# Three queues for the last stores of a decode block: block 0 through GpSimd, block 1 as two 16-row stores

## The chip, the cores and the metric

The kernel runs on one core of a Trainium2 chip. The metric is the device time of one execution in microseconds. Before the change the median of 3 runs is 263.7 us (263.6 to 263.76).

## The reference

One decode step for 8 sequences: a layer norm, attention of 32 query heads over 4 KV heads and the last 1024 cached positions, an output projection with a residual, then a second layer norm and a gated feed-forward part with its own residual. All numbers are float32.

```
W = min(4096, max(256, Sk // 4))                       # 1024
q = layernorm(x) @ wq                                  # 8 x 4096: 32 heads of 128
p = softmax(q . k[last W] * Dh**-0.5)                  # 8 query heads share one KV head
h = x + (p . v[last W]) @ wo                           # 8 x 1024
n = layernorm(h)
h2 = h + (gelu(n @ w_gate) * (n @ w_up)) @ w_down      # 8 x 1024, the output
```

## The kernel before

Every weight and cache entry is read once, 111 MB in all, in a packed order: twelve units of 8 MB go in turn into two halves of SBUF (`wbuf`), then the rest of the down projection in pieces that shrink towards the end. TensorE multiplies each chunk by a few stationary columns. Four groups of 32 PSUM partitions hold four quarters of the 1024 output columns, so the result stands as 128 partitions x 256 columns (`o_fin`): partition group j has columns 256j to 256j + 255. Of each group of 32 partitions 8 carry the eight sequences that are wanted; the host picks them out after the launch.

The end of the program matters here. The last row block of `w_down` comes in two column blocks, of 160 and 96 columns per group (`ENDS`, L32). For each, four matmuls (L472) and one VectorE add (L475) give the block's part of `o_fin`. `done[i]` is the semaphore value that says block i's add is over. `move` (L95) issues one DMA from a named engine's queue with a semaphore that counts to 16 when the data is written. The list `sent` (L486) stores the two blocks: block 0 from SyncE, block 1 from ScalarE. `EDGES` (L34) says which partitions are stored: 24 to 104, that is 80 rows, in which the wanted rows are the first 16 and the last 16.

After its store ScalarE counts up `issued` (L493). SyncE waits for that (L494), clears the semaphores of the whole program in two range clears (L498), and then waits for each store's semaphore and sets it back (L500). SyncE's last wait ends the program. An engine's queue is in order: what stands behind a waiting instruction waits as well. GpSimd's last instruction is a copy at L429 (`singles`), 12 us before the end.

Of the kernel before, what the change touches and what calls it, by code (L numbers as in the profile page):

```python
# [2 lines left out]
F32 = mybir.dt.float32  # L3
# [5 lines left out]
B = 8  # L9
D = 1024  # L10
# [6 lines left out]
QW = D // NQ  # L17
# [13 lines left out]
ENDPARTS = (2, 1)  # L31
ENDS = (160, 96)  # L32
AHEAD = 3
EDGES = ((24, 104),)  # L34
PAD = 128


# [8 lines left out]
class Flow:  # L46
# [48 lines left out]
    def move(self, name, out, src, *waits, engine="sync", sem=None):  # L95
        s = self.sem(name) if sem is None else sem
        self.start(engine, lambda e: e.dma_start(out, src), waits).then_inc(s, 16)  # L97
        return s, 16


def decode_block(nc, x, units, dn, tails, ends, outs):

    fl = Flow(nc)
    run, move = fl.run, fl.move
# [3 lines left out]
    def sb(name, *shape):  # L108
        return nc.alloc_sbuf_tensor(name, list(shape), F32).ap()
# [37 lines left out]
    def half_b(k, h=1):  # L147
        return at_mark["b", k, h]
# [5 lines left out]
    for u in range(UNITS):  # L154
        k, i = divmod(u, 2)
# [7 lines left out]
    for i, (n, sem) in enumerate(zip(PARTS, (go[0], *go_later[1:]))):  # L163
        c0 = (q0 - EARLY) * D
# [4 lines left out]
    c0 = 0  # L169
    for i, n in enumerate(ENDPARTS):  # L170
        here = move(f"we{i}", wbuf[1][:, c0:c0 + n * D], tails[i], half_b(nb - 1))
# [6 lines left out]
    blocks = []  # L178
    a = 0
    for i, (n, src) in enumerate(zip(ENDS, ends)):  # L180
        t = wbuf[1][:, c0:c0 + NQ * n]
# [8 lines left out]
        out=ident, in_=ident, compare_op=ALU.not_equal, fill=1.0, base=0,  # L190
# [14 lines left out]
    for i, g in enumerate(go_later):  # L205
        run("gpsimd", lambda e: e.memset(note[:, i:i + 1], 0.0), gives=(g, GATE[i] * (passes - 1)))

    own = sb("own", P, HB)
    own_ok = run("vector", lambda e: e.tensor_reduce(
        out=own, in_=ident.rearrange("p (a b h) -> p b a h", b=HB, h=REP), axis=AX.XY,  # L210
# [88 lines left out]
    for hf in range(2):  # L299
        done = (half_a, half_b)[hf]  # L300
# [26 lines left out]
    for hf in range(2):  # L327
        done = (half_a, half_b)[hf]
# [3 lines left out]
            out=nmax, in_=sums[hf], axis=AX.X, op=ALU.max, negate=True), done(1))  # L332
# [12 lines left out]
    for hf in range(2):  # L345
        done = (half_a, half_b)[hf]
        o_sb = sb(f"o{hf}", P, DH)
        tok = None
        for h in range(2):
            o3 = sums[hf][:, h * N:(h + 1) * N].rearrange("p (b d) -> p b d", b=HB)  # L350
            for b in range(HB):
                end = h == 1 and b == HB - 1
                out = source[:, hf * DH:(hf + 1) * DH] if end else o_sb
# [39 lines left out]
    for k, n in enumerate(SETS):  # L393
# [16 lines left out]
        t = turned[:, 0:N].rearrange("p (i m) -> p i m", m=P)  # L410
# [24 lines left out]
    for ch in range(2):  # L435
        p0 = 32 * (2 + ch)
# [31 lines left out]
    o_fin = sb("o_fin", P, QW)  # L468
    done = []
# [10 lines left out]
    with nc.body("never", valid_engines=both):  # L480
# [3 lines left out]
    nc.switch_bb("through")  # L484

    sent = [  # L486
        move(f"out{i}_{k}", outs[i][k], o_fin[p0:p1, c0:c0 + n], done[i], engine=("sync", "scalar")[i])
        for i, (c0, n, t, here) in enumerate(blocks) for k, (p0, p1) in enumerate(EDGES)
    ]


    issued = fl.sem("issued")
    nc.scalar.sem_inc(issued, 1)  # L493
    nc.sync.wait_ge(issued, 1)  # L494
    late = [s.num for s, val in sent]
    for group in ([s.num for s in fl.sems if s.num < min(late)], [issued.num]):
        assert group == list(range(group[0], group[0] + len(group)))
        nc.sync.sem_clear(range(group[0], group[-1] + 1))  # L498
    for s, val in sent:
        nc.sync.wait_ge(s, val).then_inc(s, -val)  # L500


# [86 lines left out]
```

## Time and profile before

| | us |
|---|---|
| median of 3 runs | 263.7 |
| the profiled execution | 263.75 |
| its span, first to last instruction | 262.3 |
| TensorE busy | 142.3 (54%) |
| VectorE busy | 43.8 (17%) |
| ScalarE busy | 13.5 (5%) |
| GpSimd busy | 8.6 (3%) |
| mean DMA rate | 424 GB/s |

The span is the time between the first and the last instruction of the profile; the profiled execution's own time is 1.45 us more. Over most of the span the DMA engines are busy with weights, and the compute engines follow them. A store's row in the profile shows only its issue. Its data moves later, on the DMA engines, and its semaphore counts later still; "to landing" is the time from the issue's start to that count.

### The profile page before, as it was taken

To read this page: it belongs to the slowest core of one execution; us is meant where nothing else is said; L and a number is where in the kernel's file an instruction comes from. 1 tells how busy PE (TensorE), PEld (TensorE's weight loads), DVE (VectorE), ACT (ScalarE), POOL (GpSimd) and SP (SyncE) were. 2 spreads that over 40 slices of the span, in tenths; PEclk is the share of its full clock that TensorE was granted. 3 is DMA by queue.
4 is the path that set the end of the run, shared out by engine and by line. 5 is a ranking of instruction groups with operands and counts; after the bars stand their busy time and mean duration, and the time that the engine had idled before them with its cause. 6 is when DMAs were issued, how large, how long until landed. Compare 5 with 4: busy or idle time off the path is not lost. (4 is left out here: it accounts for less than half of the span.)

```text
span 262.3 us, 2264 instructions
## 1 busy us (share of the span) xinstructions
PE 142.3 (54%) x972; PEld 45.6 (17%) x972; DVE 43.8 (17%) x115; ACT 13.5 (5%) x19; POOL 8.6 (3%) x20
## 2 busy tenths in 40 slices
PE   0025705926806937607918408827609709309996
PEld 0021201211202322102202102122103202002332
DVE  0340200240110140400410100254100300100342
ACT  1000000000030010000000200000300000200000
POOL 6000100100000000100100000000000000000000
PEclk9999975985965965975986966965957956956999
DMA  8997997999799799979979998997999899799895
GB/s 320 485 460 340 480 480 320 480 480 460 340 480 480 320 480 480 460 340 480 480 320 480 480 450 350 480 480 320 480 480 450 350 480 480 320 440 480 375 422 215
DMA packets 2800, 111.27 MB, mean 424 GB/s; under 512 B 408, under 2 KB 616, under 8 KB 880
## 3 DMA queue, kind: packets, MB, share of 16 engines
q1 hardware_dynamic: 2688, 111.20, 98.4%
q10 hardware_dynamic: 112, 0.06, 0.1%
HBM read 111.18 MB, written 0.08 MB: 424 GB/s over the span
## 5 line engine op out<-in xcount | busy, mean ns | idle before, releaser
L232 PE MATMUL sum<-w,still 128*32 128x512 f32 x832 | 116.6, 723 | 95.9 <-PEq L219 95.9
L232 PEld LDWEIGHTS sum<-w,still 128*32 128x32 f32 x832 | 32.5, 130 | 176.4 <-issue 176.3
L250 PE MATMUL turned<-ident,source 128*128 128x128 f32 x64 | 11.1, 330 | 20.8 <-PEq L219 20.8
L250 PEld LDWEIGHTS turned<-ident,source 128*128 128x128 f32 x64 | 8.8, 169 | 26.1 <-issue 26.1
L245 PE MATMUL turned<-y_sb,add 128*32 128x512 f32 x24 | 11.3, 592 | 0.9 <-PEq L219 0.9
L331 DVE TENSOR_REDUCE nmax<-sum 128x1 f32<-128x1024 f32 x2 | 2.4, 1224 | 28.4 <-PE sum L232 28.4
L406 DVE TENSOR_TENSOR up<-up,sum 128x512 f32<-128x512 f32 (+1 forms) x2 | 1.4, 685 | 34.1 <-PE sum L232 34.1
L302 DVE TENSOR_SCALAR q<-sum 128x512 f32<-128x512 f32 x2 | 1.4, 692 | 25.5 <-PE sum L232 25.5
L287 DVE COPY still<-turned 128x1024 f32<-128x1024 f32 x4 | 4.7, 1220 | 4.3 <-PE turned L250 4.3
L396 DVE TENSOR_TENSOR gate<-gate,sum 128x512 f32<-128x512 f32 (+1 forms) x2 | 1.4, 686 | 23.6 <-PE sum L232 23.6
L358 DVE SCALAR_TENSOR_TENSOR o<-sum,share,o 128x128 f32<-128x128 f32 x12 | 4.2, 351 | 4.2 <-PE sum L232 3.8
L355 DVE TENSOR_SCALAR o<-sum,share 128x128 f32<-128x128 f32 x2 | 0.7, 351 | 23.9 <-PE sum L232 23.9
L362 POOL MEMSET still<- 128x1024 f32 x2 | 1.9, 951 | 76.0 <-PE sum L232 76.0
L333 ACT ACT_TABLE_LOAD x1 | 1.3, 1283 | 60.4 <-DVE nmax L331 60.4
L245 PEld LDWEIGHTS turned<-y_sb,add 128*32 128x32 f32 x24 | 2.6, 110 | 8.7 <-issue 8.7
L307 POOL MEMSET still<- 128x1024 f32 x2 | 1.9, 956 | 45.7 <-PE sum L232 45.7
L375 DVE TENSOR_TENSOR y_sb<-y_sb,sum 128x512 f32<-128x512 f32 x1 | 0.7, 687 | 15.8 <-PE sum L232 15.8
L373 ACT COPY y_sb<-sum 128x512 f32<-128x512 f32 x1 | 0.6, 586 | 50.7 <-PE sum L232 50.7
L333 ACT ACTIVATE source<-sum,nmax 128x1024 f32<-128x1024 f32 x2 | 2.2, 1113 | 17.1 <-PE turned L250 17.1
L374 DVE TENSOR_TENSOR y_sb<-y_sb,sum 128x512 f32<-128x512 f32 x1 | 0.7, 687 | 14.3 <-PE sum L232 14.3
L318 DVE COPY still<-turned 128x16 f32<-128x16 f32 x32 | 2.7, 165 | 2.1 <-PE turned L250 2.1
L429 POOL COPY singles<-at 128x128 f32<-128x128 f32 x1 | 0.7, 664 | 71.4 <-DVE at L411 71.4
(66 smaller groups left out, 44.7 us busy)
## 6 DMA issues: line engine op xcount, KB each, us to landing
w<-dn SPq DMA_DIRECT2D x1, 6144.0 KB, 24.5
w<-dn SPq DMA_DIRECT2D x1, 2048.0 KB, 29.1
w<-tails SPq DMA_DIRECT2D x1, 1024.0 KB, 12.0
w<-tails SPq DMA_DIRECT2D x1, 512.0 KB, 12.9
w<-ends SPq DMA_DIRECT2D x1, 320.0 KB, 13.3
w<-units SPq DMA_DIRECT2D x12, 29.3
w<-ends SPq DMA_DIRECT2D x1, 192.0 KB, 13.3
out<-o_fin SPq DMA_DIRECT2D x1, 50.0 KB, 1.6
```

What stands on the lines that cost most here:

```text
L232: ins = PE.matmul(sums[i][32 * j:32 * j + 32, h * N:(h + 1) * N], still[i][:, 32 * s:32 * s + 32], wbuf[i][:, s * N:(s + 1) * N], start=(c ...
L245: ins = PE.matmul(turned[0:32, ch * N:(ch + 1) * N], add2[:, ch, :], y_sb, start=True, stop=True)
L250: ins = PE.transpose(turned[:, n * P:(n + 1) * P], source[:, n * P:(n + 1) * P], ident)
L287: run("vector", lambda e: e.tensor_copy(still[i].rearrange("p (c j m) -> p c j m", c=NC, j=NQ), turned.rearrange("p (c m) -> p c m", c=NC) ...
L302: tok = run("vector", lambda e: e.tensor_scalar(q_sb, sums[hf][:, 0:N], scale, None, op0=ALU.mult), done(0, 0))
L307: cleared.append(run("gpsimd", lambda e: e.memset(still[hf], 0.0), done(0)))
L318: run("vector", lambda e: e.tensor_copy(to[:, :, b, s, a, REP * b:REP * b + REP].rearrange("p k (h i) -> p k h i", h=2), frm[:, s, a * HB ...
L331: tok = run("vector", lambda e: e.tensor_reduce(out=nmax, in_=sums[hf], axis=AX.X, op=ALU.max, negate=True), done(1))
L333: p_ok = run("scalar", lambda e: e.activation(source, sums[hf], AF.Exp, bias=nmax, accum_out=tot), tok, at_mark["t", 1 + hf])
L358: tok = run("vector", lambda e: e.scalar_tensor_tensor(out, o3[:, b], share[hf][:, b:b + 1], o_sb, op0=ALU.mult, op1=ALU.add), tok, done(2 ...
L362: cleared[hf] = run("gpsimd", lambda e: e.memset(still[hf], 0.0), done(2))
L396: tok = run("vector", lambda e: e.tensor_add(gate[:rows], gate[:rows], sums[0][:rows, N:2 * N]), tok, half_a(4 + k))
```

## The change

`EDGES` becomes a list for each block, of partition ranges with an engine each. Block 0 (160 columns, partitions 24 to 104) is issued by GpSimd in place of SyncE. Block 1 (96 columns) is stored as two DMAs of 16 partitions, 24 to 40 from SyncE and 88 to 104 from ScalarE, in place of one of 80 partitions from ScalarE. The output tensor shrinks accordingly, and the host code that picks the rows is adapted.

At the end SyncE waits for two counts of `issued`, one from ScalarE and one from GpSimd, and then for the stores of block 1 alone. GpSimd waits for its own store, does a `dma_reset` (a drain that names this semaphore as its reset range) and clears the semaphore.

```diff
-EDGES = ((24, 104),)
+EDGES = ((((24, 104), "gpsimd"),), (((24, 40), "sync"), ((88, 104), "scalar")))
...
     sent = [
-        move(f"out{i}_{k}", outs[i][k], o_fin[p0:p1, c0:c0 + n], done[i], engine=("sync", "scalar")[i])
-        for i, (c0, n, t, here) in enumerate(blocks) for k, (p0, p1) in enumerate(EDGES)
+        move(f"out{i}_{k}", outs[i][k], o_fin[p0:p1, c0:c0 + n], done[i], engine=engine)
+        for i, (c0, n, t, here) in enumerate(blocks) for k, ((p0, p1), engine) in enumerate(EDGES[i])
     ]
...
     nc.scalar.sem_inc(issued, 1)
-    nc.sync.wait_ge(issued, 1)
+    nc.gpsimd.sem_inc(issued, 1)
+    nc.sync.wait_ge(issued, 2)
...
-    for s, val in sent:
+    for s, val in sent[1:]:
         nc.sync.wait_ge(s, val).then_inc(s, -val)
+    soft, val = sent[0]
+    soft = range(soft.num, soft.num + 1)
+    nc.gpsimd.wait_ge(sent[0][0], val)
+    nc.gpsimd.dma_reset(soft)
+    nc.gpsimd.sem_clear(soft)
```

On GpSimd (POOL) the end of the program reads as follows, with lines of the change marked +; `singles` is the copy that was the engine's last instruction, and a range clear is shown as ISA.

```order
 L381 MEMSET note 1x1 [waits tensor_done]
 L429 COPY singles<-at 128x128 [waits vector_done]
+L97 DMA out<-o_fin 80x160 [waits vector_done]
+L506 ISA [waits out0_0_done]
```

The store of block 0 and the clear of its semaphore now stand behind that copy; the drain with its reset, which is not listed, stands between them.

On SyncE (SP) the end of the program, before (-) and now (+):

```order
 L97 DMA w<-ends 128x640
 L97 DMA w<-ends 128x384
-L97 DMA out<-o_fin 80x160 [waits vector_done]
-L498 ISA [waits issued_done]
-L498 ISA
+L97 DMA out<-o_fin 16x96 [waits vector_done]
+L499 ISA [waits issued_done]
+L499 ISA
```

SyncE's store became one of block 1, and the two range clears keep their place behind it. VectorE's and TensorE's instructions are the same as before.

## Rows read from the trace of the kernel before

**Rows 1.** The page: span, and the chain that ended last, by engine

```profile
span 262.3 us, 2264 instructions
DMA 5%; PE 4%; SPq 0%; DVE 0%; issue 0%
```

**Rows 2.** Timeline of the last 3 us: start us, us, engine line op

```profile
260.01 0.37 PE L472 MATMUL sum<-w,singles 128*32 128x96 f32 x8
260.10 0.32 DVE L475 TENSOR_TENSOR o_fin<-most,fin 128x160 f32<-128x160 f32 x1 [1.18 <-PE fin L472]
260.44 0.36 SPq L97 DMA_DIRECT2D out<-o_fin  x1
260.45 0.25 DVE L475 TENSOR_TENSOR o_fin<-most,sum 128x96 f32<-128x96 f32 x1
260.74 0.36 ACTq L97 DMA_DIRECT2D out<-o_fin  x1
```

**Rows 3.** SyncE's waits at the end: us in total, times, longest us

```profile
SPq L500 <- SPq L500: 1.1, 2, 0.8
SPq L498 <- ACTq L493: 0.3, 1, 0.3
```

**Rows 4.** SyncE's and ScalarE's last instructions by line: ns min/median/max, first and last start

```profile
L500 SPq EVENT_SEMAPHORE  x2: 17/17/17, 262.1 to 262.3; - x2
L498 SPq EVENT_SEMAPHORE_RANGE_CLEAR  x2: 25/42/58, 261.2 to 261.3; - x2
L493 ACTq EVENT_SEMAPHORE  x1: 17/17/17, 261.1 to 261.1; - x1
```

**Rows 5.** Stretches of the end; last two columns: DMA busy share, GB/s

```profile
261.20:261.30 0.10, 0.00 (x0) 0.00 (x0) 0.00 (x0) 0.00 (x0) 0.00 (x0) 1.00 0.00 0
...
261.30:261.40 0.10, 0.00 (x0) 0.00 (x0) 0.00 (x0) 0.00 (x0) 0.00 (x0) 1.00 0.49 142
...
261.90:262.00 0.10, 0.00 (x0) 0.00 (x0) 0.00 (x0) 0.00 (x0) 0.00 (x0) 1.00 0.03 8
```

**Rows 6.** DMA queues from 260.5 to 262.3 (packets, MB, share); stores with us to landing

```profile
q1 hardware_dynamic: 96, 0.05, 10.7%
q10 hardware_dynamic: 96, 0.03, 7.4%
...
out<-o_fin SPq DMA_DIRECT2D x1, 50.0 KB, 1.6
out<-o_fin ACTq DMA_DIRECT2D x1, 30.0 KB, 1.6
```

**Rows 7.** Issues of other DMAs: ns min/median/max, first and last start

```profile
L97 SPq DMA_DIRECT2D w<-units x12: 327/328/421, 0.7 to 205.6; - x12
...
L97 ACTq DMA_DIRECT2D x_sb<-x x1: 1207/1207/1207, 1.7 to 1.7; - x1
```

**Rows 8.** GpSimd's groups by shape: busy us, mean ns, idle before

```profile
L196 POOL MEMSET source<- 128x1024 f32 x1 | 1.0, 951 | 0.0
...
L193 POOL MEMSET y_sb<- 128x512 f32 x1 | 0.5, 524 | 0.0
...
L381 POOL MEMSET note<- 1x1 f32 x1 | 0.1, 88 | 46.9 <-PE turned L250 46.9
```

**Rows 9.** GpSimd's drain at the program's start: ns

```profile
L554 POOLq DRAIN  x1: 186/186/186, 0.3 to 0.3; - x1
```

**Rows 10.** GpSimd's first affine_select by line; then GpSimd's timeline (start, us)

```profile
L189 POOLq MODIFY_POOL_CONFIG  x2: 1/1/1, 1.8 to 1.8; - x2
...
L189 POOL TENSOR_SCALAR_AFFINE_SELECT ident<-ident x1: 292/292/292, 1.9 to 1.9; 128x128 f32<-128x128 f32 x1
...
1.62 0.20 POOL L188 MEMSET ident<- 128x128 f32 x1
1.89 0.29 POOL L189 TENSOR_SCALAR_AFFINE_SELECT ident<-ident 128x128 f32<-128x128 f32 x1
...
248.69 0.66 POOL L429 COPY singles<-at 128x128 f32<-128x128 f32 x1 [71.43 <-DVE at L411]
```

More of the change, by code (lines that the diff above doesn't have):

```diff
@@ L558 @@
     }
-    held = sum(p1 - p0 for p0, p1 in EDGES)
-    out = nc.dram_tensor("out", (held * QW,), F32, kind="ExternalOutput").ap()
+    held = [sum(p1 - p0 for (p0, p1), _ in edges) for edges in EDGES]
+    out = nc.dram_tensor("out", (sum(h * n for h, n in zip(held, ENDS)),), F32, kind="ExternalOutput").ap()
     outs, f0 = [], 0
-    for n in ENDS:
+    for n, edges in zip(ENDS, EDGES):
         outs.append([])
-        for p0, p1 in EDGES:
+        for (p0, p1), _ in edges:
             size = (p1 - p0) * n
@@ L580 @@
     flat = r.results[0]["out"].reshape(-1)
-    got, f0 = np.empty((held, QW), np.float32), 0
-    for a, b in zip(cuts, cuts[1:]):
-        size = held * (b - a)
-        got[:, a:b] = flat[f0:f0 + size].reshape(held, b - a)
-        f0 += size
-    two = 2 * B
-    got = np.stack([got[0:B], got[B:two], got[held - two:held - B], got[held - B:]], 1)
-    return own(got).reshape(B, 1, D)
+    got, f0 = [], 0
+    for n, h in zip(ENDS, held):
+        part = flat[f0:f0 + h * n].reshape(h, n)
+        f0 += h * n
+        two = 2 * B
+        got.append(np.stack([part[0:B], part[B:two], part[h - two:h - B], part[h - B:]], 1))
+    return own(np.concatenate(got, 2)).reshape(B, 1, D)
```

## The prediction

> **What bounds the kernel now.** I read the page's header and its chain of waits first, then the timeline of the last three microseconds, then who waits for whom on SyncE (SP). The chain that ended last [rows 1] is weight traffic, then the last weight columns, two small matmul groups and the last add; its final step is a store, and a store's own time is not in that chain. So I followed the end by hand. VectorE finishes block 0 of the result at 260.10 + 0.32 = 260.42 us and block 1 at 260.45 + 0.25 = 260.70 [rows 2]. SP issues the store of block 0 from 260.44, ScalarE (ACT) that of block 1 from 260.74. After that no compute engine works: the last 1.6 us of the span belong to two stores. SP's two last waits show it [rows 3]: 0.8 us for the first store and 0.3 us for the second, the second one ending the span at 262.3 [rows 4]. Block 0 is known to be written at about 262.07, block 1 at 262.3, each 1.6 us after the start of its issue [rows 6].
>
> A store thus falls into three pieces. Issue: 0.36 us on SP and on ACT [rows 2]. Then silence until data moves: the DMA engines stand still until 261.3 [rows 5], some 0.87 us after SP's issue began. Then the packets, and after the last one (about 261.95) some 0.35 us until SP sees the count. Each store has 96 packets on 16 engines, 80 rows and 16 more, so 5 rows and 1 more on each engine. They took 10.7% and 7.4% of a 1.8 us window [rows 6]: 0.107 x 1.8 x 16 / 96 = 32 ns a packet for block 0 and 22 ns for block 1.
>
> **The change part by part.** All engines do the same up to 260.70; only what follows differs.
>
> *Block 1, now on two queues.* Where ACT stored 80 rows of 96 numbers, SP and ACT store 16 rows each, both after the add that ends at 260.70. SP has no earlier store to issue, so its queue is free. The issue: 128 rows took 327 ns and 80 rows 359 [rows 2, 7], so rows hardly set it and I count 0.36 unchanged. Data begins 0.87 us after the start of an issue; 16 rows are 1 per engine instead of 5, so 4 x 22 ns = 0.09 us go, and more if block 0's packets, now later, no longer share the engines. From 260.72: + 0.87 + 2 packets (0.05) + 0.35 = 261.99 at best, and 262.3 if nothing is gained. The gain on this branch is 0 to 0.31 us. The two issues start together; before, they overlapped by 0.06 us without either growing, so I count no delay there, and 0.36 us (262.66) if the second has to wait for the first to end.
>
> *Block 0, now on GpSimd (POOL).* POOL has been idle since its copy, which began at 248.69 [rows 10], so it starts with the add's end, at 260.44. No row of before shows a DMA issued by POOL, so its issue must be bounded. From below: the cheapest POOL instruction, 0.09 us [rows 8], which would make it 0.27 us shorter than on SP. The middle: POOL's small copy, 0.66 [rows 10], and its dearest memset, 0.95 [rows 8]. Farther: ACT's first DMA of this run took 1.21 us for 8 rows against 0.36 for its later one with 80 rows [rows 2, 7]; POOL's store is the first that POOL issues. Farthest: if each of 80 rows cost one cheapest instruction, 80 x 0.09 = 7.0 us. I take 1.21, the only row of a queue's first issue of a few rows. What follows the issue I take from SP's store: from 260.80 to 262.07, 1.27 us, with the same 80 rows and 5 per engine.
>
> *The ending, moved to POOL.* One of SP's two waits goes (17 ns, nothing). POOL instead waits for its store, drains with a reset, and clears one semaphore. A drain on POOL took 186 ns [rows 9], a range clear 25 to 58 ns [rows 4]. That is 0.23 us behind the landing, where SP needed 17 ns. Nothing hides it if POOL is last. Below, it is the clear alone, 0.03; above, I allow one more drain, 0.4.
>
> *The issue count.* SP now also waits for POOL's increment before it clears the other semaphores. The clears end at about 261.35 today and SP then stands 0.8 us for its store [rows 3, 4]. With POOL's issue at 1.21 the increment comes at 261.65, and the clears are over by 261.75, before the stores of SP and ACT land (261.99 at best). So it costs nothing; if the issue takes longer than about 1.4 us it delays SP, but POOL is then later still.
>
> *The sum.* POOL's branch: 260.44 + 1.21 + 1.27 + 0.23 = 263.15. SP's and ACT's branch: 261.99 to 262.3. POOL is last, by about a microsecond, and the span grows from 262.3 to 263.15, by 0.85 us. The profiled execution took 263.75, so 1.45 us lie outside its span and I leave them: 264.6. The median of the three runs shown is 263.7, 0.05 lower; that gives 264.55, and I write 264.5.
>
> *A rule weighed against a row.* The trace has no POOL store, only SP's 1.6 us for the same 50 KB [rows 6]. The Trainium skill, page "DMA: Bandwidth & Descriptors", section on the anatomy of one DMA on the gpsimd path, fits the whole of such a DMA as 2.0 us plus bytes over 436 GB/s; by that estimate 51,200 bytes take 2.12 us, 0.5 us above the SP row. The sum by it would be 260.44 + 2.12 + 0.23 = 262.79, 0.49 us later than now, and 264.2 us in all: just inside what cannot be told from no change. No run yet shows which holds.
>
> **The rivals.** About 0.2% of 263.7, 0.53 us, is what a measurement of this kernel can tell from no change.
>
> *POOL's issue costs no more than its other instructions (not slower).* For it: POOL's instructions take between 0.09 and 0.95 us, and affine_select was as quick as 0.29 us at its first use [rows 8, 10]. Against it: writing out 80 rows is a different kind of work. With 0.09 the branch ends at 260.44 + 0.09 + 1.27 + 0.23 = 262.03; with 0.66 at 262.60; it decides below 0.89 us, where the end is 262.83. The end lies between 262.0 and 262.83: 263.4 to 264.2 us, with 0.66 us 264.0. The skill's fit above falls into this case.
>
> *POOL's issue is paid row by row, or its first DMA needs something fetched (much slower).* At 0.09 us a row it is 7.0 us and the span ends at 268.9: 270.3 us; a third of that gives 265.7. For it: a store by software has 80 rows to write. Against it: POOL's memset does 512 columns more in 0.43 us [rows 8], so small pieces of work need not cost an instruction each. On something fetched, the trace has MODIFY_POOL_CONFIG at 1.8 us and the affine_select at 1.89, right behind the memset that ended at 1.82 [rows 10]. The Trainium skill, "GPSIMD Engine Reference", section on instruction dispatch, has the first call of freshly loaded code pay some 6 us after such an instruction; by that the sum would be near 270.5, but here no gap follows it, so I give it little.
>
> *The smaller stores gain more than the noise (faster).* The SP and ACT branch ends at 261.99 at best, 0.31 us or 0.12% below now, and POOL's at 262.03 at best. For faster by 0.53 us both would have to beat their bounds, for instance if the 0.87 us before the first packet or the 0.35 us after the last depended on the number of rows. Nothing in the rows says so; 263.1 would be its time.
>
> **How the numbers follow.** Forecast, POOL last by 0.5 to 1.9 us (264.2 to 265.6): 0.50. POOL's issue cheap (263.4 to 264.2): 0.34, of which 0.01 falls just above the bound. Row by row or fetched (above 265.6): 0.11. Faster: 0.05. So slower by over 0.2% is 0.50 + 0.11 + 0.01 = 0.62, within 0.2% 0.33, faster 0.05. The range takes the first two cases nearly whole, 263.5 to 265.6, and leaves out some 0.17.
>
> **What would show it.** In the profile after: POOL's issue row with its duration (1.2 us, or below 0.9 for the rival, above 2.5 for the row-by-row case); POOL's drain and clear as the last instructions of the span; SP's last wait over by 262.3 at the latest while POOL still waits; the store of block 0 moving its packets later than those of SP and ACT. It is wrong if SP's waits end the span, or if the drain with its reset costs much more than 0.19 us. Should SP's issue be 0.3 us late or twice as long, the two issues stand in each other's way.

## The result, and the profile after

| | before | after |
|---|---|---|
| median of 6 runs, us | 263.64 | 264.65 |
| lowest to highest, us | 263.58 to 263.76 | 264.59 to 264.88 |
| profiled execution, us | 263.75 | 264.74 |
| its span, us | 262.3 | 262.9 |
| outside the span, us | 1.45 | 1.84 |

The kernel became slower by 0.4%: the ratio is 1.0039, interval 1.0026 to 1.0052, about 1.0 us. Only some 0.5 us of it are in the span. In the six runs after, the span is 262.7 to 263.0 us (median 262.8), and 1.81 to 1.95 us (median 1.87) lie outside it. Before, the profiled execution had 1.45; the medians of the same kernel further down are 1.35 and 1.36. (Spans are listed to 0.1 us, so the difference of a single execution is good to 0.05 us.)

The end of the timeline after, with start, duration, engine, line and operation; it answers to [rows 2]:

```profile
260.17 0.32 DVE L475 TENSOR_TENSOR o_fin<-most,fin 128x160 f32<-128x160 f32 x1 [1.19 <-PE fin L472]
260.51 0.26 DVE L475 TENSOR_TENSOR o_fin<-most,sum 128x96 f32<-128x96 f32 x1
260.79 0.36 SPq L97 DMA_DIRECT2D out<-o_fin  x1
260.79 0.65 POOL L97 DMA_DIRECT2D out<-o_fin  x1 [11.69 <-DVE o_fin L475]
260.79 0.39 ACTq L97 DMA_DIRECT2D out<-o_fin  x1
```

The two adds stand 0.06 to 0.07 us later than before. That is scatter between executions: in the experiments below that edit only the very end, the first add begins at anything from 260.05 to 260.26. Block 0's add is over at 260.49, but GpSimd's store begins at 260.79, together with those of block 1. Its issue takes 0.65 us.

The last synchronising instructions after, by line, with ns and the first and last start; they answer to [rows 4] and [rows 9]:

```profile
L494 POOLq EVENT_SEMAPHORE  x1: 17/17/17, 260.8 to 260.8; - x1
...
L501 SPq EVENT_SEMAPHORE  x2: 17/17/17, 262.2 to 262.4; - x2
...
L505 POOLq DRAIN  x1: 66/66/66, 262.8 to 262.8; - x1
...
L506 POOLq EVENT_SEMAPHORE_RANGE_CLEAR  x1: 48/48/48, 262.9 to 262.9; - x1
```

SyncE is through at 262.4, where it was at 262.3. GpSimd ends the program half a microsecond later. Its drain with reset took 66 ns. The first line is GpSimd's count of `issued`. In the chain that ended last it stands ahead of the store, though it comes behind it in the program:

```profile
260.77 0.02 POOLq L494
260.79 0.00 issue
260.79 0.65 POOL out L97
```

The DMA queues after, from 260.5 to 263, and the stores' landing times; they answer to [rows 6]:

```profile
q0 software_dynamic: 32, 0.05, 6.9%
q1 hardware_dynamic: 32, 0.01, 1.4%
q10 hardware_dynamic: 32, 0.01, 1.3%
issues: line engine op xcount, KB each, median us to landing
out<-o_fin POOLq DMA_DIRECT2D x1, 50.0 KB, 1.9
out<-o_fin SPq DMA_DIRECT2D x1, 6.0 KB, 1.4
out<-o_fin ACTq DMA_DIRECT2D x1, 6.0 KB, 1.6
```

GpSimd's store lands 1.9 us after its issue began, at 262.69, which is 2.20 us after the add. SyncE's store of the same 50 KB landed 1.6 us after its issue and 1.65 after the add. The stretches after (the last two columns are DMA busy share and GB/s) answer to [rows 5]:

```profile
261.60:261.70 0.10, 0.00 (x0) 0.00 (x0) 0.00 (x0) 0.00 (x0) 0.00 (x0) 1.00 0.14 27
261.70:261.80 0.10, 0.00 (x0) 0.00 (x0) 0.00 (x0) 0.00 (x0) 0.00 (x0) 1.00 0.49 89
261.80:261.90 0.10, 0.00 (x0) 0.00 (x0) 0.00 (x0) 0.00 (x0) 0.00 (x0) 1.00 0.05 8
261.90:262.00 0.10, 0.00 (x0) 0.00 (x0) 0.00 (x0) 0.00 (x0) 0.00 (x0) 1.00 0.00 0
262.00:262.10 0.10, 0.00 (x0) 0.00 (x0) 0.00 (x0) 0.00 (x0) 0.00 (x0) 1.00 0.93 288
```

First come the 32 small packets of each hardware queue, then nothing, then from 262.0 GpSimd's: 1.2 us after its issue began, against 0.87 on SyncE before.

### The profile page after: what moved, and what is told of

Its sections match the earlier page's. It is cut to its first block, busy times and chain, and to the rows that moved or that the text cites. A ratio compares the mean times of both kernels' runs of the same rounds, so it can differ in the third digit from the quotient of the medians.

```text
span 262.9 us, 2268 instructions
## 1 busy us (share of the span) xinstructions
PE 144.7 (55%) x972; PEld 45.7 (17%) x972; DVE 43.8 (17%) x115; ACT 13.5 (5%) x19; POOL 9.3 (4%) x21
## 5 line engine op out<-in xcount | busy, mean ns | idle before, releaser
L232 PE MATMUL sum<-w,still 128*32 128x512 f32 x832 | 119.7, 740 | 93.6 <-PEq L219 93.6
L232 PEld LDWEIGHTS sum<-w,still 128*32 128x32 f32 x832 | 33.1, 132 | 176.5 <-issue 176.4
L250 PE MATMUL turned<-ident,source 128*128 128x128 f32 x64 | 10.4, 314 | 20.8 <-PEq L219 20.8
```

The lines of the kernel that those rows point to most:

```text
L232: ins = PE.matmul(sums[i][32 * j:32 * j + 32, h * N:(h + 1) * N], still[i][:, 32 * s:32 * s + 32], wbuf[i][:, s * N:(s + 1) * N], start=(c ...
L250: ins = PE.transpose(turned[:, n * P:(n + 1) * P], source[:, n * P:(n + 1) * P], ident)
```

## The experiments

Two things were open: the 0.4 us outside the span, which no step of the prediction had, and the 0.30 us before GpSimd's issue. Theory A says that the end of the program costs more behind GpSimd's last instruction than behind SyncE's. The rivals were that any program with a software store (one that GpSimd issues; the profile lists its queue as software_dynamic) pays it, and that the small stores themselves cost time. All runs had 11 executions of the kernel, but for e8 with one, which is read for its timeline. "Outside" is the median of time less span; the kernel before, measured beside each, had 1.35 or 1.36 (ranges within 1.28 to 1.46).

| | median us | before | ratio, interval | span | outside |
|---|---|---|---|---|---|
| e1_hw_split | 263.86 | 263.73 | 1.0003, 0.9993 to 1.0012 | 262.5 | 1.37 |
| e2_early_soft | 263.67 | 263.73 | 0.9995, 0.9986 to 1.0004 | 262.3 | 1.34 |
| e3_pool_last | 264.27 | 263.73 | 1.0018, 1.0009 to 1.0027 | 262.4 | 1.85 |
| e4_sync_last | 264.08 | 263.73 | 1.0012, 1.0003 to 1.0021 | 262.8 | 1.32 |
| e5_act_last | 263.88 | 263.67 | 1.0012, 1.0003 to 1.0021 | 262.4 | 1.49 |
| e6_dve_last | 263.89 | 263.67 | 1.0010, 1.0000 to 1.0019 | 262.4 | 1.49 |
| e7_pe_last | 264.07 | 263.67 | 1.0015, 1.0006 to 1.0024 | 262.4 | 1.67 |
| e8_add_between | 264.77 | 263.67 | one execution | 263.1 | 1.67 |
| e9_pool_before_sync | 263.98 | 263.66 | 1.0013, 1.0004 to 1.0022 | 262.3 | 1.63 |
| e10_small_block0 | 264.14 | 263.66 | 1.0017, 1.0008 to 1.0026 | 262.8 | 1.33 |

**e1_hw_split: no GpSimd, block 1 still in two.**

```diff
-EDGES = ((((24, 104), "gpsimd"),), (((24, 40), "sync"), ((88, 104), "scalar")))
+EDGES = ((((24, 104), "sync"),), (((24, 40), "sync"), ((88, 104), "scalar")))
```

> Block 0 stays on SyncE (80 rows), block 1 goes as 16 rows each on SyncE (behind block 0's issue) and ScalarE; GpSimd does nothing at the end. Theory (the loss of 1.0 us is all GpSimd's branch: its store lands later, and the end of the program costs some 0.4 us more outside the span): the end is back with SyncE, span 262.0 to 262.3 and 1.45 us outside it, 263.3 to 263.7 us in all. Rival (the small stores, or two issues at once, cost time themselves): 264.0 us or more.

It is level with the kernel before, so the loss is GpSimd's branch, its store and the ending together. The median is 0.13 us above the kernel before and outside the theory's 263.3 to 263.7: the forecast gain of the small stores did not come. The timeline of its end:

```profile
260.65 0.83 SPq L97 DMA_DIRECT2D out<-o_fin  x2
260.65 0.26 DVE L475 TENSOR_TENSOR o_fin<-most,sum 128x96 f32<-128x96 f32 x1
260.94 0.38 ACTq L97 DMA_DIRECT2D out<-o_fin  x1
```

SyncE's second issue stands behind its first one and is over only at 261.48, while ScalarE's is over at 261.32. What 16 rows save (1.5 us to landing instead of 1.6) goes into that queue.

**e2_early_soft: the kernel before and a software store in the middle.**

```diff
     run("gpsimd", lambda e: e.memset(note[:, 7:8], 0.0), at_mark["t", 5], gives=(go_fold, 2))
+    fl.start("gpsimd", lambda e: e.dma_start(extra, idle[24:40, 0:160]), [idle_ok]).then_inc(soft, 16)
+    nc.gpsimd.wait_ge(soft, 16)
+    nc.gpsimd.dma_reset(range(soft.num, soft.num + 1))
+    nc.gpsimd.sem_clear(range(soft.num, soft.num + 1))
```

> The kernel before, and in addition a store of 16 x 160 zeros by GpSimd to a spare place of the output in the middle of the program (about 177 us), with its wait, reset and clear right behind it; the end is that of before. Theory A (the 0.4 us outside the span come because GpSimd's instruction is the last of the program): 263.7 us, 1.45 us outside the span. Rival B (a program with a software store pays them wherever the store stands): 264.1 us, 1.85 us outside the span.

No cost, in the span or outside it: this small software store and its reset were free in the middle of the program, though the data took 9.7 us to land beside the weights. Two lines of its timeline on GpSimd:

```profile
176.73 0.09 POOL L382 MEMSET note<- 1x1 f32 x1 [46.89 <-PE turned L251]
177.28 0.64 POOL L383 DMA_DIRECT2D out<-idle  x1 [0.46 <-issue]
```

Issuing 16 rows (10 KB) took 0.64 us, 80 rows (50 KB) 0.65, so between these sizes neither rows nor bytes set it. Both stores made 32 packets; whether packets set it is not shown, and no run has a second GpSimd store to compare with the first. And the store began 0.46 us after the memset with nothing to wait for.

**e3_pool_last: no software store, GpSimd ends the program.**

```diff
-    for s, val in sent:
+    for s, val in sent[:1]:
         nc.sync.wait_ge(s, val).then_inc(s, -val)
+    s, val = sent[1]
+    nc.gpsimd.wait_ge(s, val)
+    nc.gpsimd.sem_clear(range(s.num, s.num + 1))
```

> The kernel before with its two stores on SyncE and ScalarE, but GpSimd, not SyncE, waits for ScalarE's store and clears its semaphore, so that GpSimd's clear is the last instruction; there is no software store. Theory A (GpSimd last costs outside the span): span 262.35, 1.85 us outside it, 264.1 to 264.2 us. Rival B (the software store pays it): span 262.35, 1.45 outside, 263.7 to 263.8 us.

The span is that of before, and 0.49 us come in outside it (1.85 against 1.36). This settles it for theory A against the software store: one wait and one clear moved from SyncE to GpSimd cost half of what the change cost, with no such store in the program. Its last instructions:

```profile
L500 SPq EVENT_SEMAPHORE  x1: 17/17/17, 262.0 to 262.0; - x1
...
L503 POOLq EVENT_SEMAPHORE_RANGE_CLEAR  x1: 48/48/48, 262.3 to 262.3; - x1
```

**e4_sync_last: the change, but SyncE ends the program; reset and clear stand at its start.**

```diff
+    nc.gpsimd.dma_reset(range(soft.num, soft.num + 1))
+    nc.gpsimd.sem_clear(range(soft.num, soft.num + 1))
...
     for s, val in sent[1:]:
         nc.sync.wait_ge(s, val).then_inc(s, -val)
-    soft, val = sent[0]
-    soft = range(soft.num, soft.num + 1)
-    nc.gpsimd.wait_ge(sent[0][0], val)
-    nc.gpsimd.dma_reset(soft)
-    nc.gpsimd.sem_clear(soft)
+    nc.sync.wait_ge(*sent[0])
```

> The changed kernel, but SyncE waits for GpSimd's store as the last instruction of the program, and the reset and clear of that store's semaphore stand at the start of the program on GpSimd. Theory A (GpSimd last costs outside the span): the span ends at about 262.7, 1.45 us outside it, 264.1 to 264.2 us. Rival B (the software store pays it): span 262.7, 1.85 us outside, 264.55 us.

As theory A had it: 1.32 us outside, and what is left, 0.35 us, is the later landing. SyncE's three last waits:

```profile
L504 SPq EVENT_SEMAPHORE  x2: 17/17/17, 262.3 to 262.5; - x2
...
L505 SPq EVENT_SEMAPHORE  x1: 17/17/17, 262.9 to 262.9; - x1
```

The third, for GpSimd's store, comes 0.4 us behind the second. So the 1.0 us of the change divide into 0.35 for the later landing (e4), 0.49 behind GpSimd's last instruction (e3) and some 0.15 that are left, by difference, for its drain and clear.

**e5_act_last, e6_dve_last, e7_pe_last: the other engines as the last.** The edit of e5; e6 and e7 have `nc.vector` and `nc.tensor`.

```diff
-    for s, val in sent:
-        nc.sync.wait_ge(s, val).then_inc(s, -val)
+    nc.sync.wait_ge(*sent[0]).then_inc(sent[0][0], -16)
+    nc.scalar.wait_ge(*sent[1]).then_inc(sent[1][0], -16)
```

> The kernel before, but ScalarE waits for its own store and sets its semaphore back as the last instruction; SyncE waits only for the store of block 0. Theory (each engine has its own price for being last; GpSimd's is 0.5 us above SyncE's): nothing says what ScalarE's is; if GpSimd alone is dear, 1.36 us outside the span and 263.7 us in all. Rival (SyncE is the cheap one, every other engine is dear): 1.85 us outside, 264.2 us.

> As e5_act_last, but VectorE waits for ScalarE's store and sets the semaphore back, last in the program. If GpSimd alone is dear: 1.36 us outside the span, 263.7 us. If SyncE alone is cheap: 1.85 us outside, 264.2 us.

> As e5_act_last, but TensorE waits for ScalarE's store and sets the semaphore back, last in the program. If GpSimd alone is dear: 1.36 us outside the span, 263.7 us. If SyncE alone is cheap: 1.85 us outside, 264.2 us.

Neither form held: 1.49, 1.49 and 1.67 us outside. In each the engine's own wait is the last instruction, at 262.3 (ScalarE) and 262.4 (VectorE, TensorE). The time outside the span thus differs by engine; call it the engine's tail. SyncE's is the shortest, GpSimd's the longest, TensorE's in between. One thing stays open: GpSimd ends with a range clear in every run in which it is late, the other engines with a wait that sets the semaphore back. How much of GpSimd's tail belongs to the engine and how much to that last instruction no run separates.

**e8_add_between: an add between the two.**

```diff
+        if c0 == 0:
+            run("vector", lambda e: e.tensor_add(sb("between", P, N), rest, sums[0][:, 0:N]), mark=False)
```

> The changed kernel with one more VectorE add of 128x512 (0.69 us, into an unused tile) between the adds of block 0 and of block 1. It tells apart why GpSimd's issue began 0.28 us after block 0's add, at the very end of block 1's add. If GpSimd's queue needs that time to start a store, the issue still begins 0.26 to 0.30 us after block 0's add, while VectorE works. If GpSimd cannot start while VectorE works, it begins 0.7 us after it or later, at the end of the added add or of block 1's. In the first case the span ends where block 1's stores end, about 0.5 us later than in the changed kernel at most; in the second up to 0.7 us later.

```profile
260.18 0.32 DVE L475 TENSOR_TENSOR o_fin<-most,fin 128x160 f32<-128x160 f32 x1 [1.18 <-PE fin L472]
260.42 0.68 DVE L478 TENSOR_TENSOR between<-rest,sum 128x512 f32<-128x512 f32 x1
260.80 0.65 POOL L97 DMA_DIRECT2D out<-o_fin  x1 [12.37 <-DVE o_fin L475]
261.02 0.25 DVE L475 TENSOR_TENSOR o_fin<-most,sum 128x96 f32<-128x96 f32 x1
...
L508 POOLq EVENT_SEMAPHORE_RANGE_CLEAR  x1: 48/48/48, 262.9 to 262.9; - x1
...
L503 SPq EVENT_SEMAPHORE  x2: 17/17/17, 262.9 to 263.1; - x2
```

GpSimd starts 0.30 us after block 0's add while VectorE works on, so it does not wait for VectorE; the agreement with the end of block 1's add was chance. Nor does GpSimd learn late that VectorE is done: in the kernel before, its copy [rows 10] began at 248.69, 0.06 us after the VectorE copy that it waits for was over:

```profile
248.07 0.56 DVE L411 COPY at<-turned 128x384 f32<-128x384 f32 x1 [1.28 <-PE turned L250]
```

Together with e2 this makes it a starting time of GpSimd's store: 0.28 to 0.30 us behind an add, 0.46 us in e2. What it consists of is not shown.

**e9_pool_before_sync: GpSimd late, but not last.**

```diff
-    for s, val in sent:
-        nc.sync.wait_ge(s, val).then_inc(s, -val)
+    s, val = sent[0]
+    nc.gpsimd.wait_ge(s, val)
+    nc.gpsimd.sem_clear(range(s.num, s.num + 1))
+    nc.sync.wait_ge(*sent[1]).then_inc(sent[1][0], -16)
```

> The kernel before with its two stores, but GpSimd waits for the store of block 0 and clears its semaphore (at about 262.1), and SyncE waits for the store of block 1 alone, as the last instruction of the program (262.35). Theory A (every engine has its own tail behind its last instruction, GpSimd 1.85 us, SyncE 1.36, and the end is the latest of them): GpSimd sets the end though it is not last, 262.1 + 1.85 = 263.95 us, some 1.6 us outside the span. Rival B (only the engine of the last instruction counts): 1.36 us outside the span, 263.7 us.

```profile
L501 POOLq EVENT_SEMAPHORE_RANGE_CLEAR  x1: 48/48/48, 262.1 to 262.1; - x1
...
L502 SPq EVENT_SEMAPHORE  x1: 17/17/17, 262.3 to 262.3; - x1
```

263.98 us where 263.95 was expected. The last instruction is SyncE's, yet GpSimd's tail of 1.85 us, counted from its clear at 262.1, reaches further than SyncE's 1.36 from 262.3. So the end of the execution is the latest of the engines' last instructions, each with its own tail. It fits e8 too: there SyncE ends the span at 263.1 and its tail would give 264.5; GpSimd's clear is over at 262.95, with its tail 264.80, and 264.77 was measured.

**e10_small_block0: e4_sync_last with more lead for GpSimd's store.**

```diff
-ENDS = (160, 96)
+ENDS = (64, 192)
```

> The kernel e4_sync_last (GpSimd's store awaited by SyncE, reset at the start) with blocks of 64 and 192 columns in place of 160 and 96, so that GpSimd's store can start earlier. If GpSimd's store is late only for want of a lead (2.2 us from block 0's add to its landing), block 0's add ends at about 260.15, its store lands at about 262.35, and the whole takes 263.6 to 263.8 us, level with the kernel before and 0.3 below e4_sync_last. If the store's latency grows or block 1's larger add costs more than the lead gives, 264.0 us or more.

The 263.6 to 263.8 us did not come; it took 264.14 us. Its end:

```profile
259.71 0.37 ACT L464 COPY most<-acc 128x256 f32<-128x256 f32 x1 [17.23 <-PE acc L449]
260.19 0.22 DVE L478 TENSOR_TENSOR o_fin<-most,fin 128x64 f32<-128x64 f32 x1 [1.05 <-ACT most L464]
...
260.71 0.65 POOL L97 DMA_DIRECT2D out<-o_fin  x1 [11.40 <-DVE o_fin L478]
260.81 0.35 DVE L478 TENSOR_TENSOR o_fin<-most,sum 128x192 f32<-128x192 f32 x1 [0.40 <-PE sum L475]
261.19 0.36 SPq L97 DMA_DIRECT2D out<-o_fin  x1
261.20 0.39 ACTq L97 DMA_DIRECT2D out<-o_fin  x1
...
L504 SPq EVENT_SEMAPHORE  x2: 17/17/17, 262.7 to 262.9; - x2
```

Block 0's add could not start before ScalarE's copy, so it ended at 260.41 and not at 260.15. Its store starts 0.48 us ahead of the others, lands 1.8 us after the start of its issue, at about 262.5, and no longer ends the program: SyncE's waits for the two stores of block 1 do, at 262.7 and 262.9, and the wait for GpSimd's store behind them finds it landed. Block 1's larger matmuls and add put those later, and what GpSimd's store gained is lost there. No version found here beats the kernel before; e1 and e2 are level with it.

## Why the prediction was right, and where it was not

It said slower, by GpSimd's store, and 264.5 us; 264.65 were measured. The direction and the place are shown: without GpSimd's store and ending (e1) the loss is gone. That the number came within 0.15 us is luck: the size came out by two errors that cancel.

*GpSimd's issue, 1.21 us.* Too high. It is 0.65, behind a start of 0.28 to 0.30 us that the sum did not have: 0.95 us from the add to the end of the issue, against 0.02 + 1.21. ScalarE's first DMA was a poor stand-in, and it was not the only first issue on record: none of SyncE's twelve issues in [rows 7], its first included, took over 0.42 us. The 0.66 us of GpSimd's copy [rows 10] would have met the issue alone, but nothing here says that the two have a common cause.

*From the end of the issue to landing, 1.27 us.* Measured 262.69 less 261.44, 1.25. The part that was taken from SyncE's store held.

*Drain and clear, 0.23 us.* Measured some 0.2 from landing to the end of the clear. The sum held, its parts did not: the drain took 66 ns, not 186, and the clear 48 ns; the other 0.1 us lie between the landing, the drain and the clear.

So the span's end was put at 263.15; it is 262.9, or 262.83 without the 0.07 us by which the adds stood later. By the span alone the growth would be 0.5 us, at the border to the cheap-issue rival, which gave 262.83 as its upper end. The Trainium skill, page "DMA: Bandwidth & Descriptors", section on the anatomy of one DMA on the gpsimd path, was nearer than my sum here: its fit gives 2.12 us by that estimate, and the trace has 2.20 from the add to the landing, or 1.9 from the start of the issue.

*The 1.45 us outside the span, "I leave them".* This is the step that failed. They depend on which engine ends, and with GpSimd they are 1.85 to 1.87 (e3, the change). The missing 0.4 to 0.5 us made up for the issue that was too dear.

*Block 1, gain of 0 to 0.31 us.* SyncE's and ScalarE's small stores landed 1.4 and 1.6 us after issue, and SyncE was through at 262.4, no earlier than before: the gain was nothing, the range's lower end. Data began as reckoned, 0.87 us after the issue. But the packets took some 0.2 us, to about 261.85, where 0.05 were reckoned, and ScalarE's store counted at about 262.4, some 0.5 us behind them, not 0.35. Why is not shown. The two issues together cost ScalarE 0.39 instead of 0.36 us.

*The issue count, free.* Right, for another reason: GpSimd's increment came at 260.77, before its store's issue began, and not at 261.65, and SyncE's clears ran at 261.3 as before.

*The row-by-row rival* falls: 16 and 80 rows take 0.64 and 0.65 us to issue. No fetch showed either: the store began 0.30 us after the add. The 6 us that the Trainium skill, "GPSIMD Engine Reference", section on instruction dispatch, has for the first call of freshly loaded code did not show.

## What to carry to other kernels

A span is not the whole time: when an edit changes which engine executes the last instruction, ask what lies behind that engine's end, and let the engine with the shortest tail (here SyncE) do the last waits and clears. GpSimd's queue is no spare third queue for a last small store: here its store landed 0.55 us later after the data was ready than SyncE's. A smaller one in the middle of the program cost nothing.

## What the runs showed of the hardware

- Time outside the span by the engine that ends the program: SyncE 1.32 to 1.37 us, ScalarE and VectorE 1.49, TensorE 1.67, GpSimd 1.85 to 1.87 (with a range clear as its last instruction). Whether part of it lies ahead of the first instruction the profile does not say; the differences lie at the end, since e3, e5, e6, e7 and e9 edit nothing else.
- GpSimd's store of 80 rows of 640 bytes made 32 packets, two on each of 16 engines, where SyncE's of the same rows made 96. At 6.9% of 2.5 us on 16 engines that is 86 ns a packet in the mean, so an engine worked 0.17 us on it, against 6 x 32 ns = 0.19 for SyncE's. The later landing comes from the start and the issue (0.95 us from the add to the end of the issue, against 0.38 on SyncE), not from the moving of data.
- A semaphore increment that stands behind GpSimd's store in the program was carried out before the store's issue began (260.77 against 260.79 to 261.44): it does not show that the store has been issued.
